# Attention and feed-forward on one core: q and k transposed from the layout in which they were loaded

## The chip, the cores and the metric

The kernel runs on 1 core of one Trainium2 chip. The metric is the device time of one execution in microseconds (us), the median of several runs; lower is better. The time before is 370.84 us, the median of 3 runs (370.76 to 371.65).

## What is computed

Squared-ReLU attention over 8 batches of 12 heads, 448 positions of 64 numbers each, and behind it a feed-forward layer with an exact GELU on the 3,584 tokens. Inputs and output are float32.

```python
# q, k, v: (8, 12, 448, 64); w_in: (768, 2048); w_out: (2048, 768)
scores = (1 / np.sqrt(64)) * np.matmul(q, k.transpose(0, 1, 3, 2))
attn = np.maximum(scores, 0.0) ** 2 / 448
a = np.matmul(attn, v)
x = np.ascontiguousarray(a.transpose(0, 2, 1, 3)).reshape(8 * 448, 12 * 64)
h = x @ w_in
g = 0.5 * h * (1.0 + erf(h / np.sqrt(2)))
out = g @ w_out
```

## The kernel before

Five engines work side by side: TensorE (PE) multiplies, VectorE (DVE) and ScalarE (ACT) empty PSUM, GpSimd (POOL) issues the loads that turn float32 into bfloat16, SyncE (SP) issues stores and DMA transposes. A small scheduler inside the kernel decides, while the program is built, in which order each engine gets its instructions. It keeps estimates of durations and of free buffers, and takes at each step the operation that can start first. The beginning of the program is fixed by a long list, `ORDER`.

Names: `b` is the batch (0 to 7), `g` one of three groups of four heads, `i` one of seven blocks of positions of k, `c` one of four blocks of 112 positions of q.

The scores need q and k with the 64 numbers of a head along the partitions, so both are transposed. For batches 0 and 1, TensorE transposes them by way of PSUM. For batches 2 to 7 a DMA transpose does it, on SyncE's queue, from the tiles `pq` and `pk`, in which the columns of two heads already lie side by side, so that one head lands on partitions 0 to 63 and the other on 64 to 127. Batch 2 is loaded plainly and brought into that layout by VectorE; batches 3 to 7 are loaded into it directly, in pieces of 64 numbers.

```python
# ... batch 2: VectorE permutes what was loaded
def permute_k(copy, g, src):
    copy(get_p()[1][:, g].rearrange("p (i e d) -> p e i d", e=2, d=D),
         src.rearrange("p e (i d) -> p e i d", d=D))
# ... batches 3 to 7: loads straight into the permuted layout (issued from GpSimd)
def add_wide(b):
    def k_fn(e):
        def fn():
            to = get_p()[1].rearrange("p g (i e d) -> e p g i d", e=2, d=D)
            src = kv_view(k, b, 0, G).rearrange("p (g e) (i d) -> e p g i d", e=2, d=D)
            for g in range(G):
                nc.gpsimd.dma_start(to[e][:, g], src[e][:, g])
        return fn
    # ... q the same way, in four parts of three loads; v in one load
# ... DMA transposes of one batch: three for k, four for q
def add_T_dma(b, after):
    for g in range(G):
        # ... nc.sync.dma_start_transpose(kT[:, g], pk[:, g])
    for c in range(NC):
        # ... nc.sync.dma_start_transpose(qT[:, :, bass.ts(c, KC)], pq[:, c, :])
# ... a tiny copy on GpSimd that reads qT: it holds the next batch's loads back
def add_gate(b):
    def fn(e):
        nc.gpsimd.tensor_copy(gate, get_T(b)[0][:, 0, ::KC])
```

A block of scores is four matmuls, one in each quadrant of the array, into one two-bank PSUM tile of a pool of three (`w_pp`). ReLU empties it (ScalarE or VectorE), VectorE squares, and after seven blocks 28 matmuls multiply by v.

```python
ps = box["ps"] = w_pp.tile([128, 2, NB], F32, tag="w", name="ps")
for e in range(2):
    r = slice(64 * e, 64 * e + 64)
    for j in range(2):
        nc.tensor.matmul(
            ps[64 * j : 64 * j + 64, e, x * w : x * w + w],
            kT[r, g, i * 128 + 64 * j : i * 128 + 64 * j + 64],
            qT[r, 2 * g + j, cols(half)], start=True, stop=True)
```

Matmuls of the feed-forward (`psh`, then `pso`, and in the last part `pb`) stand between the attention's in TensorE's order. The second weights come in three loads by rows, `WOUTS = (4, 6, 6)` of sixteen row blocks, the first of them ahead of the transposes of batch 2. VectorE forms sums of their quarters (`t_sb`), with which seven products do the work of eight. `LEADS = {3: 4}` puts four feed-forward runs ahead of batch 3's attention.

Of the kernel before, what the change touches and what calls it, by code (L numbers as in the profile page):

```python
# [8 lines left out]
F32 = mybir.dt.float32  # L9
# [4 lines left out]
KC = 112  # L14
# [9 lines left out]
FF = 2048  # L24
KD = DM // 128
KF = FF // 128
ND = DM // 2
NG = B * S // 256
# [3 lines left out]
WOUTS = (4, 6, 6)  # L32
# [3 lines left out]
T_TWO = 0.72  # L36
# [8 lines left out]
DMA_FREE = 4.54  # L45
# [7 lines left out]
LEADS = {3: 4}  # L53
# [3 lines left out]
NEAR = 0.5  # L57
# [4 lines left out]
WIDE = 2.0  # L62
# [13 lines left out]
G0 G1 G2 G3 G4 G5 A10 D13 G6 A16 P11 P14 G7 D12 A15 P17 G8 D18 P21 P39 D22 P33 P36 A34 D40  # L76
P19 D20 A37 P23 G9 P42 P48 D24 P54 A43 D35 A49 P51 D44 P25 D38 A52 D41 G117 A55 D53 P45 D50
A26 D47 A46 P57 D56 P69 P66 A58 D70 P27 G118 A67 P29 D59 P63 G119 A28 D71 P60 A64 G120 D68
P78 D61 A62 P75 A79 D65 P81 P31 D30 A76 D80 P96 G121 D32 A97 P72 D77 G122 A82 D98 P129 G123
D74 A73 P90 D130 P84 P108 A91 G124 D83 P131 A85 D109 P93 P141 D132 A94 D92 P102 D95 P105  # L80
P111 A103 D86 P143 D110 G125 A106 D104 P99 A112 D107 G126 A144 P87 D100 A101 D113 A142 P157
P114 D88 G127 A158 D89 P133 D115 A116 G128 P135 D159 A134 P160 P163 D136 P166 A164 P145 D167
A161 D165 P253 A146 D168 D162 P169 P172 G147 A254 P175 A173 D170 P245 G148 A176 D171 P255
A246 D177 G149 D174 P184 P187 A256 P196 A185 G150 D188 P137 P139 A138 P178 D197 G151 A140
D186 P193 P211 G152 D180 P247 A212 G153 D213 P249 A248 D179 A194 D198 G154 P263 A250 D195
D229 G155 P223 P220 A264 D189 P190 S235 A224 D221 P265 G156 A191 D225 P267 A266 D192 D222
P199 P217 A268 P214 D231 A218 P257 S236 D215 A200 D219 P259 A258 D216 D201 P181 P208 A260
P205 D230 A209 P261 D182 P251 D183 A262 D210 A206 D233 P202 A252 S237 D207 D232 P226 D234
A203 D204 S238 S239 P269
# [17 lines left out]
class Scheduler:  # L107
# [70 lines left out]
    def commit(self, est, op, eng, dur, lat):  # L178
# [5 lines left out]
        if isinstance(lat, tuple):  # L184
            t = max(self.dma, est + dur + 1.0)
            self.dma = t + lat[0] / 390e3
            op.done = self.dma + DMA_LAT
            self.landed += [op.done] * lat[1]
        else:
            op.done = est + lat  # L190
# [68 lines left out]

    def place(self, fixed):  # L260
# [14 lines left out]
        while rest or any(fixed.values()):  # L275
# [7 lines left out]
            for e, v in fixed.items():  # L283
                if v and not (e == "PE" and by.get("PE")):
                    tops.append(self.pick(v[:1]))
# [11 lines left out]
def kernel(  # L297
# [34 lines left out]
    q32 = natpool.tile([KC, 4, HC * D], F32, tag="pq", name="q32")  # L332
    k32 = natpool.tile([128, 2, NK * D], F32, tag="pk", name="k32")

    def get_nat(b):
        if b not in nq:

            tq, tk = ("pq", "pk") if b == 1 else ("nq", "nk")
            nq[b] = natpool.tile([KC, H, NC * D], BF16, tag=tq, name="nq")
            nk[b] = natpool.tile([128, HP, NK * D], BF16, tag=tk, name="nk")  # L340
            vt[b] = vpool.tile([128, HP, NK * D], BF16, tag="v", name="v_sb")

# [4 lines left out]
    def load_q(b, g0, g1, c0=0, c1=NC):  # L347
        get_nat(b)
        nc.gpsimd.dma_start(  # L349
            nq[b][:, 4 * g0 : 4 * g1, c0 * D : c1 * D], q_view(b, g0, g1, c0, c1)  # L350
        )
# [18 lines left out]
    def load_wout(kf):  # L370
        w = moe_w_out.rearrange("(kf p) d -> p kf d", p=128)
        nc.gpsimd.dma_start(wout_sb[:, kf, :], w[:, kf, :])

    pqk = []

    def get_p():
        if not pqk:  # L380
            pqk.append(natpool.tile([KC, NC, DM], BF16, tag="pq", name="pq"))
            pqk.append(natpool.tile([128, G, NK * 128], BF16, tag="pk", name="pk"))
        return pqk
# [4 lines left out]
    def get_T(b):  # L388
        if b not in qkT:
            qkT[b] = (  # L390
                tpool.tile([128, HP, S], BF16, tag="qT", name="qT"),
                tpool.tile([128, G, NK * 128], BF16, tag="kT", name="kT"),
            )
        return qkT[b]

# [24 lines left out]
    Pq, Pk, Tq, Tk = {}, {}, {}, {}  # L420
# [3 lines left out]
    def war(b):  # L424

        old = [o for (bb, *_), o in list(Pq.items()) + list(Pk.items()) if bb == b - 1]
        c = {1: -1, 2: 0}.get(b, b - 1)
        old += [o[0] for (bb, *_), o in list(Tq.items()) + list(Tk.items()) if bb == c]
        return old

    def add_k(b, g0, g1):
# [4 lines left out]
        o = dma(fn, (g1 - g0) * 4 * S * 256, war(b))  # L436
# [3 lines left out]
    def add_q(b, g0, g1, c0=0, c1=NC):  # L440
# [3 lines left out]
        o = dma(lambda: load_q(b, g0, g1, c0, c1), n, war(b))  # L444
# [4 lines left out]
    def add_v(b, g0, g1):  # L449
        def fn():  # L450
            get_nat(b)
            nc.gpsimd.dma_start(vt[b][:, 2 * g0 : 2 * g1], kv_view(v, b, g0, g1))  # L452

        old = [o for (bb, *_), o in AV.items() if bb == b - 3]
# [4 lines left out]
    def add_wide(b):  # L459


        def k_fn(e):
            def fn():
                to = get_p()[1].rearrange("p g (i e d) -> e p g i d", e=2, d=D)
                src = kv_view(k, b, 0, G).rearrange("p (g e) (i d) -> e p g i d", e=2, d=D)
                for g in range(G):
                    nc.gpsimd.dma_start(to[e][:, g], src[e][:, g])  # L467

            return fn

        def q_fn(e, j):
            def fn():
                to = get_p()[0].rearrange("p c (g j e d) -> j e g p c d", j=2, e=2, d=D)
                src = q[b].rearrange("(g e j) (p c) d -> j e g p c d", e=2, j=2, c=NC)
                for g in range(G):
                    nc.gpsimd.dma_start(to[j][e][g], src[j][e][g])  # L476

            return fn

        def v_fn():  # L480
            vt[b] = vpool.tile([128, HP, NK * D], BF16, tag="v", name="v_sb")
            nc.gpsimd.dma_start(vt[b], kv_view(v, b, 0, G))

        n = G * 4 * S * 256
        ks = [dma(k_fn(e), WIDE * n / 2, war(b), G) for e in range(2)]
        qs = [dma(q_fn(e, j), WIDE * n / 4, war(b), G) for e in range(2) for j in range(2)]
        old = [o for (bb, *_), o in AV.items() if bb == b - 3]
        o = dma(v_fn, n, old)
        ops = Both(ks), Both(qs)
        for g in range(G):  # L490
            ld_v[b, g] = [o]
            Pk[b, g] = ops[0]
            for c in range(NC):
                Pq[b, g, c] = ops[1]

    class Both:


        def __init__(self, ops):
            self.ops = ops  # L500

        @property
        def done(self):
            ends = [o.done for o in self.ops]
            return None if None in ends else max(ends)

    def add_load(b, g0=0, g1=G):
        if b > 2:
            return add_wide(b)
        add_k(b, g0, g1)  # L510
        add_q(b, g0, g1)
        add_v(b, g0, g1)
# [8 lines left out]
    def add_wout(i):  # L521
        m = sum(WOUTS[:i])
        kf = slice(m, m + WOUTS[i])
        ld_wout[i] = dma(lambda: load_wout(kf), DM * 128 * WOUTS[i] * 4)


    def permute_k(copy, g, src):

        copy(
            get_p()[1][:, g].rearrange("p (i e d) -> p e i d", e=2, d=D),  # L530
            src.rearrange("p e (i d) -> p e i d", d=D),
        )

    def permute_q(copy, g, c0, c1, src):

        dst = get_p()[0][:, c0:c1, 256 * g : 256 * g + 256].rearrange(
            "p c (j e d) -> e p j c d", j=2, d=D
        )
        for e in range(2):
            copy(dst[e], src[:, 2 * e : 2 * e + 2].rearrange("p j (c d) -> p j c d", d=D))  # L540

    def add_pk(b, g0, g1, after=(), bias=0.0):
        for g in range(g0, g1):
            deps = ld_k[b, g] + list(after)
            deps += [Tk[max(b - 1, 1), x, i][0] for x in range(G) for i in range(NK)]
            Pk[b, g] = sch.add(
                (("DVE", 0.31, 0.43),),
                lambda e, g=g: permute_k(V.tensor_copy, g, nk[b][:, 2 * g : 2 * g + 2]), deps,
                bias=bias,
            )  # L550

    def add_pq(b, g0, g1, c0=0, c1=NC, after=(), bias=0.0):
        for g in range(g0, g1):
            deps = [ld_q[b, g, c] for c in range(c0, c1)] + list(after)
            deps += [Tq[max(b - 1, 1), g, c][0] for c in range(c0, c1)]
            if b == 2:
                deps += [Tq[1, x, c][0] for x in range(G) for c in range(NC)]
            d = 2 * (0.07 + (c1 - c0) * 128 / 3840)

            def fn(e, g=g):  # L560
                permute_q(
                    V.tensor_copy, g, c0, c1, nq[b][:, 4 * g : 4 * g + 4, c0 * D : c1 * D]
                )

            op = sch.add((("DVE", d, d + 0.12),), fn, deps, bias=bias)
            for c in range(c0, c1):
                Pq[b, g, c] = op
# [89 lines left out]

    xT, hT = {}, {}
# [790 lines left out]
```

## Time and profile before

| | |
|---|---|
| time, median of 3 | 370.84 us (370.76 to 371.65) |
| span of the profiled run | 368.9 us |
| granted TensorE clock | 0.999 |
| PE / DVE / ACT / POOL busy | 358.9 / 288.3 / 200.8 / 108.0 us |
| packets of the loads' queue, share of 16 DMA engines | 58.6% |
| packets of the queue of stores and transposes | 26.8% |

How to read it: busy time is the time in which an engine worked on an instruction. The records of matmuls overlap and their ends are modelled, so a busy TensorE can still lose time; the distance from one start to the next shows that better. PEld is the load of stationary operands, beside the matmuls. In a list of waits, the engine and line that waited stand left of the arrow and what released them right of it, with total us, number of times and the longest. `psh L800` is the tile that is written and the line of the kernel. Idle time of an engine that is not the bottleneck costs nothing.

### The profile page before, as it was taken

The numbers are of one execution on the slowest core, as the hardware profiler recorded it, in microseconds if no ns is written. First come the engines' busy times: TensorE is split into PE (matmuls) and PEld (weight loads), VectorE is DVE, ScalarE is ACT, GpSimd is POOL, SyncE is SP. The second block draws the span as 40 slices with busy tenths as digits, with TensorE's granted clock in tenths as the row PEclk, the third lists the DMA queues.
The fourth block names the chain that finished last, engine by engine and source line by source line (L and its number), as shares of the span: only waits on it lengthen the run. The fifth ranks groups of instructions, "written<-read, shape, count | busy, mean of one in ns | idle before, by whom it ended". The sixth has DMA issues, their size and how long they took to land.

```text
span 368.9 us, 8544 instructions
## 1 busy us (share of the span) xinstructions
PE 358.9 (97%) x3557; PEld 222.1 (60%) x3557; DVE 288.3 (78%) x493; ACT 200.8 (54%) x308; POOL 108.0 (29%) x149
## 2 busy tenths in 40 slices
PE   8799999999999999999999999999999999999994
PEld 7566645455544455544455545457886897688663
DVE  2998991789868978987699888888998658665862
ACT  4988865664447845677755588853440353044200
POOL 8666401726087096097095000000000000000000
PEclk9999999999999999999999999999999999999999
DMA  9999999999999999999999960003002301310233
GB/s 174 196 200 204 202 189 134 173 171 131 244 135 167 160 85 172 209 163 154 146 93 133 205 117 2 3 0 87 2 0 88 85 2 29 109 36 2 85 85 88
DMA packets 114166, 42.98 MB, mean 116 GB/s; under 512 B 92816, under 2 KB 110672, under 8 KB 114128
## 3 DMA queue, kind: packets, MB, share of 16 engines
q0 software_dynamic: 74992, 22.47, 58.6%
q1 hardware_dynamic: 38768, 19.46, 26.8%
q8 instruction: 28, 0.46, 0.5%
q10 hardware_dynamic: 368, 0.51, 0.4%
q14 instruction: 10, 0.08, 0.1%
HBM read 45.61 MB, written 11.01 MB: 153 GB/s over the span
## 4 chain that ended last, share of the span: by engine, by line
PE 87%; DMA 4%; DVE 4%; ACT 2%; POOL 1%; issue 1%; DVEq 0%; POOLq 0%; ACTq 0%
PE pso L1108 32%; PE psh L800 24%; PE pb L942 13%; PE ps L686 8%; PE pav L746 6%; PE pso L1203 3%; DMA v_sb<-in_v_dram 2%; DVE a_sq L707 2%; DMA nk<-in_k_dram 2%; ACT a_sq L698 2%; POOL nk L434 0%; POOL v_sb L452 0%; POOL nq L349 0%; PE tp L580 0%; DVE a_sq L700 0%
## 5 line engine op out<-in xcount | busy, mean ns | idle before, releaser
L698 ACT ACTIVATE a_sq<-ps 128x896 bf16<-128x896 f32 (+1 forms) x136 | 117.4, 914 | 44.6 <-PE ps L686 44.5
L707 DVE TENSOR_TENSOR a_sq<-a_sq 128x896 bf16<-128x896 bf16 (+1 forms) x169 | 97.5, 617 | 7.5 <-ACT a_sq L698 7.2
L800 PE MATMUL psh<-xT,win_sb 128*128 128x448 bf16 (+1 forms) x516 | 96.6, 340 | 0.1
L800 PEld LDWEIGHTS <-win_sb 128*128 128x128 bf16 x516 | 47.8, 98 | 45.5 <-issue 10.2
L810 ACT ACTIVATE h_sb<-psh 128x448 bf16<-128x448 f32 x80 | 43.9, 549 | 24.1 <-PE psh L800 23.9
L1108 PEld LDWEIGHTS <-s_sb 128*128 128x128 bf16 x424 | 40.6, 98 | 27.0 <-issue 2.2
L700 DVE TENSOR_SCALAR a_sq<-ps 128x896 bf16<-128x896 f32 x33 | 35.9, 1090 | 18.3 <-PE ps L686 17.8
L686 PE MATMUL ps<-qT,kT 64*64 64x448 bf16 (+1 forms) x756 | 47.3, 336 | 2.2 <-ACT qT L402 0.6
L976 DVE TENSOR_TENSOR part<-pb,part 128x448 f32<-128x448 f32 x60 | 34.6, 619 | 18.4 <-PE pb L942 18.4
L476 POOL DMA_DIRECT2D pq<-in_q_dram x60 | 41.8, 704 | 10.1 <-DVE a_sq L707 6.4
L1108 PEld LDWEIGHTS <-h_sb 128*128 128x128 bf16 x312 | 29.9, 98 | 21.1 <-issue 2.5
L1108 PE MATMUL pso<-wout_sb,s_sb 128*128 128x384 bf16 (+2 forms) x216 | 38.1, 320 | 0.3 <-DVE osb L1142 0.3
L1108 PE MATMUL pso<-wout_sb,h_sb 128*128 128x384 bf16 x208 | 38.1, 326 | 0.0
L1108 PE MATMUL pso<-t_sb,s_sb 128*128 128x384 bf16 x208 | 38.1, 326 | 0.0
L746 PE MATMUL pav<-a_sq,v_sb 64*64 64x448 bf16 (+1 forms) x756 | 36.8, 330 | 0.7 <-ACT a_sq L698 0.4
L686 PEld LDWEIGHTS <-kT 64*64 64x64 bf16 x756 | 18.3, 105 | 24.2 <-issue 17.4
L985 ACT ACTIVATE h_sb<-part 128x448 bf16<-128x448 f32 x36 | 19.8, 578 | 19.9 <-DVE part L976 19.8
L467 POOL DMA_DIRECT2D pk<-in_k_dram x30 | 28.9, 966 | 1.5 <-issue 0.9
L746 PEld LDWEIGHTS <-v_sb 64*64 64x64 bf16 x756 | 21.1, 107 | 13.0 <-issue 2.3
L942 PEld LDWEIGHTS <-win_sb 128*128 128x128 bf16 x288 | 27.6, 98 | 2.2 <-issue 0.4
L1142 DVE TENSOR_TENSOR osb<-pso,p_sb 128x384 f32<-128x384 f32 x39 | 21.7, 556 | 8.2 <-PE pso L1108 5.7
L400 DVE CAST xT<-pav 128x448 bf16<-128x448 f32 (+1 forms) x43 | 23.7, 583 | 4.6 <-PE pav L746 3.9
(62 smaller groups left out, 292.0 us busy)
## 6 DMA issues: line engine op xcount, KB each, us to landing
pk<-in_k_dram POOLq DMA_DIRECT2D x30, 112.0 KB, 4.4
pq<-in_q_dram POOLq DMA_DIRECT2D x60, 56.0 KB, 5.0
v_sb<-in_v_dram POOLq DMA_DIRECT2D x5, 672.0 KB, 9.1
out_dram<-osb SPq DMA_DIRECT2D x8, 336.0 KB, 3.0
wout_sb<-in_moe_w_out_dram POOLq DMA_DIRECT2D x2, 1152.0 KB, 12.1
v_sb<-in_v_dram POOLq DMA_DIRECT2D x9, 224.0 KB, 8.8
out_dram<-osb SPq DMA_DIRECT2D x7, 288.0 KB, 3.4
out_dram<-osb SPq DMA_DIRECT2D x8, 240.0 KB, 3.1
```

Source lines behind the costliest of these rows:

```text
L467: nc.gpsimd.dma_start(to[e][:, g], src[e][:, g])
L476: nc.gpsimd.dma_start(to[j][e][g], src[j][e][g])
L686: nc.tensor.matmul(ps[64 * j : 64 * j + 64, e, x * w : x * w + w], kT[r, g, i * 128 + 64 * j : i * 128 + 64 * j + 64], qT[r, 2 * g + j, co ...
L698: A.activation(ar, ps, AF.Relu, scale=c_att)
L700: V.tensor_scalar(ar, ps, c_att, 0.0, op0=mybir.AluOpType.mult, op1=mybir.AluOpType.max,)
L707: V.tensor_mul(box["a2"][:, :, :used], ar, ar)
L746: nc.tensor.matmul(pav[0][o2 : o2 + 64, e, :w], vt[b][r, 2 * g + e, bass.ts(i, D)], box["a2"][r, e, o : o + w], start=(i == 0), stop=(i == ...
L800: nc.tensor.matmul(ph[:, x * n : x * n + n], win_sb[:, kd, bass.ts(m + x, 128)], xT[b][:, kd, c], start=(kd == 0), stop=(kd == KD - 1),)
L810: A.activation(h_ring()[:, m : m + nm, o + c.start : o + c.stop], box[0][:, :S].rearrange("p (x n) -> p x n", x=nm), AF.Gelu,)
L942: nc.tensor.matmul(bank[name][:, y, z * HS : z * HS + HS], w[:, k, bass.ts(mm, 128)], right()[:, k], start=first and k == 0 and z == 0, st ...
L976: V.tensor_add(get(to), ps(name), get(other))
L1108: nc.tensor.matmul(box[bank][:, n0:n1], left()[:, kf], right[:, kf, n0:n1], start=bool(need) and kf == 0, stop=kf == K2 - 1, skip_group_ch ...
```

## The change

For batches 2 to 7 the permuted tiles disappear. q and k are loaded plainly, and the DMA transpose reads them as they lie. A block of 128 columns then holds two neighbouring 64-number pieces of the same head, not one piece each of two heads. For k that decides only which piece of which head lands on which half of the partitions. For q, each piece has to be there on both halves, since a piece of k on the upper half needs a q on the upper half. So q is transposed twice, the second time from an offset of 64 columns, with zeros at the ends, into slots that alternate.

Loads and transposes go in turn by groups of four heads: group `g` of the next batch is loaded once group `g` of this one has been transposed. The second weights come in column pieces: first the right half of all rows, then the left half in two steps, all after batch 2's transposes. Tiles move: the two float32 tiles of the start and the inputs of batch 1 use buffers that are free early, and the sums of weights take the space of transposed tiles. The scheduler gets a rule by which a feed-forward run may go ahead of an attention step that would wait, and `LEADS` becomes empty.

```diff
-WOUTS = (4, 6, 6)
+WOUTS = (
+    (slice(ND, DM), [slice(0, KF)]),
+    (slice(0, ND), [slice(0, 4), slice(8, 12)]),
+    (slice(0, ND), [slice(4, 8), slice(12, 16)]),
+)
-LEADS = {3: 4}
+LEADS = {}
 # ... in the scheduler
+    def pick_pe(self, v):
+        top = self.pick(v[:1])
+        wait = math.inf if top is None else top[1] - self.free["PE"]
+        if v[0].mode == "F" or wait <= (PULL if self.mode == "F" else PULL_IN):
+            return top
+        nxt = next((o for o in v if o.mode == "F"), None)
+        other = nxt and self.pick([nxt])
+        if other and other[1] - self.free["PE"] <= PULL and other[1] < self.free["PE"] + wait:
+            return other
+        return top
 # ... permute_k, permute_q, add_pk, add_pq, add_wide are deleted
 # ... in add_T_dma
+        def slots_of(n, o, k):
+            return lambda: get_T(b)[0].rearrange("p (s t) -> p s t", t=KC)[
+                :, 2 * n + o : 2 * (n + k) + o - 1 : 2]
+        def q_src(n, o, k):
+            return lambda: nq[b][:, 128 * n + D * o : 128 * (n + k) + D * o]
+        n0, odd = 0, None
         for g in range(G):
+            op = turn(k_dst(g), k_src(g), list(ld_k[b, g]))
             # ...
+            n = 8 * g + 9
+            even = turn(slots_of(8 * g, 1, 8), q_src(8 * g, 1, 8), lands)
             # ...
+            odd = turn(slots_of(n0, 0, n - n0), q_src(n0, 0, n - n0), lands + beyond)
+            n0 = n
 # ... in the scores
+                            if b < 2:
+                                moving = q_rows(b)[r, 2 * g + j, cols(half)]
+                            else:
+                                n = 4 * (4 * g + 2 * ((2 * i + e) // NK) + j) + 1 - e
+                                moving = qT[r, n * KC : n * KC + S]
 # ... in the order of the program
-    add_load(3)
+    for g in range(G):
+        add_load(3, g, g + 1)
+    add_v(3, 0, G)
 # ...
             if b + 2 < B:
-                add_gate(b + 1)
-                add_load(b + 2)
+                for g in range(G):
+                    add_gate(b + 1, g)
+                    add_load(b + 2, g, g + 1)
+                add_v(b + 2, 0, G)
```

## The prediction

> **What bounds the kernel now.** I read the page's first two parts first, to see which engine is full and where. The columns of the first part are busy time, its share of the span, and instructions; the digits of the second are tenths of a fortieth of the span.
>
> ```profile
> PE 358.9 (97%) x3557; PEld 222.1 (60%) x3557; DVE 288.3 (78%) x493; ACT 200.8 (54%) x308; POOL 108.0 (29%) x149
> ...
> PE   8799999999999999999999999999999999999994
> ...
> DMA  9999999999999999999999960003002301310233
> ```
>
> Two things look full: TensorE to the end, and DMA up to 0.58 of the span. They have to be told apart, because the change is nearly all DMA. The waits of TensorE, longest first in total, decide it:
>
> ```profile
> PE ps L686 <- ACT qT L402: 0.6, 1, 0.6
> ...
> PE tp L580 <- DMA nk<-in_k_dram: 0.4, 1, 0.4
> PE pso L1108 <- DVE osb L1142: 0.3, 1, 0.3
> ...
> PE tp L608 <- DMA nq<-in_q_dram: 0.3, 1, 0.3
> ```
>
> No matmul of the attention waits for a DMA transpose (kT<-pk or qT<-pq), and the two waits for loads, 0.7 us together, are on the TensorE transposes of the first two batches, which the change leaves alone. So the full DMA engines are hidden. The last transposes of the seventh and eighth batch land at 183.3 and 216.5 us (landing times of the transposes), and their first score matmuls run at 190.8 and 221.4 us (chain of waits): 7.5 and 4.9 us in hand. The tightest is the fifth batch: 128.8 against 131.5.
>
> A busy TensorE is not yet one at its peak, so I looked for what is left in the spacing of matmuls, by the timeline of TensorE (start, length, what):
>
> ```profile
> 65.02 0.57 PE L686 MATMUL ps<-qT,kT 64*64 64x448 bf16 x8
> 65.53 1.31 PE L800 MATMUL psh<-xT,win_sb 128*128 128x448 bf16 x6
> 66.76 0.57 PE L686 MATMUL ps<-qT,kT 64*64 64x448 bf16 x8
> 67.27 3.58 PE L800 MATMUL psh<-xT,win_sb 128*128 128x448 bf16 x18
> 70.78 0.76 PE L686 MATMUL ps<-qT,kT 64*64 64x448 bf16 x12
> 71.47 3.58 PE L800 MATMUL psh<-xT,win_sb 128*128 128x448 bf16 x18
> ```
>
> From start to start, 6 full matmuls take 1.23 us and 18 take 3.51, so one takes 2.28/12 = 0.190 and leaving the run costs 3.51 - 18 x 0.190 = 0.09. Eight quadrant matmuls take 0.51 and twelve 0.69, so four (one block of scores) take 0.18 and a visit to the quadrants costs 0.51 - 2 x 0.18 = 0.15 on top. A switch to attention and back is thus about 0.24 us; that is kept by both kernels. The real holes are few:
>
> ```profile
> 96.63 1.52 PE L746 MATMUL pav<-a_sq,v_sb 64*64 64x448 bf16 x28
> 98.50 1.46 PE L1108 MATMUL pso<-wout_sb,s_sb 128*128 128x384 bf16 x8 [0.34 <-DVE osb L1142]
> ```
>
> ```profile
> 151.10 1.49 PE L746 MATMUL pav<-a_sq,v_sb 64*64 64x448 bf16 x28
> 152.42 0.87 PE L686 MATMUL ps<-qT,kT 64*64 64x448 bf16 x8
> 153.22 0.50 PE L1108 MATMUL pso<-t_sb,s_sb 128*128 128x384 bf16 x2
> ```
>
> In the first the 28 matmuls last from 96.63 to 98.50, 1.87 us, where the other runs of 28 take 1.32 plus about 0.1 of a switch: 0.43 lost. In the second eight score matmuls take 153.22 - 152.42 = 0.80 instead of the 0.48 that they take at 76.71 after the same predecessor: 0.32 lost, while ScalarE empties three score tiles in a row and no PSUM buffer is free. The same shape stands at 203.35, 232.95 and 243.68. Together 0.43 + 4 x 0.32 = 1.7 us. That is all that TensorE loses to waits after 60 us. Before 30 us it has more gaps (25.6 busy of 30), in a part that stays as it is.
>
> **What the Trainium skill says.** "Perfetto Trace Analysis", Identifying the Most-Contended Engine, warns that matmul busy time says little about distance from the peak; hence the spacing above, not the 97%. "TensorE: Matmul & The Clock Gate", Back-to-back issue gap, gives N/2.4 + 2.5 ns for one warm matmul, 189 ns for N = 448; the trace agrees with 190, so nothing is to be had inside a run. "DMA: Bandwidth & Descriptors", Specifications, puts full line rate at 512 B and more per piece. The trace agrees in kind: a 128 B packet takes 32 ns and an 896 B one 88 (medians of the packet records), 4.0 against 10.2 bytes per ns. The same page, DMA Transpose (X-bar), has such transposes issued from Sync or Scalar only; here all are on SyncE's queue, in order with the stores, so more of them also means more issue time there.
>
> **The change part by part.**
>
> Matmuls: the changed kernel as built has the same 3,557 matmuls in the same shapes. Query slots are 448 contiguous columns as before, so each matmul should cost the same. Work: 0.
>
> DVE: the three permutes pk<-nk and six pq<-nq of the third batch go.
>
> ```profile
> L540 DVE COPY pq<-nq 112x512 bf16<-112x512 bf16 x6 | 1.4, 287 | 0.0
> ...
> L529 DVE COPY pk<-nk 128x896 bf16<-128x896 bf16 x3 | 1.2, 385 | 0.0
> ```
>
> 1.4 + 1.2 = 2.6 us, all between 40 and 60 us, where TensorE is busy 20.0 of 20 us: 0 on the path.
>
> Loads of the last five batches: the 128 B pieces go.
>
> ```profile
> pk<-in_k_dram POOLq DMA_DIRECT2D x30, 112.0 KB, 4.4
> pq<-in_q_dram POOLq DMA_DIRECT2D x60, 56.0 KB, 5.0
> ...
> qT<-pq SPq DMA_TRANSPOSE x24, 3.8
> ...
> kT<-pk SPq DMA_TRANSPOSE x18, 6.8
> ```
>
> The packet records hold 53,760 packets of 128 B, 112.8 us of all 16 engines, 22.6 us a batch. After: k in 768 pieces of 896 B at 88 ns and q in 1,344 of 512 B at 60 ns, over 16 engines 4.2 + 5.0 = 9.2 us. Saved 13.4 us of engine time a batch. GpSimd issues 6 loads of about 0.73 us where it issued 6 of 0.97 and 12 of 0.70: 4.4 for 14.2 us. None of it is on the path.
>
> Transposes: per batch 3 of 7 blocks and 4 of 6, 45 blocks, become 3 of 7, then 8 + 9 + 8 + 8 + 8 + 8 = 49 for q, 70 blocks in 9 instructions. The 32,256 packets of 256 B take 60.0 us, 10.0 a batch; times 70/45 that is 15.6, so +5.6 us; two more issues at 1.3 us on SyncE. Net DMA per batch: -13.4 + 5.6 = -7.8 us. More slack, where slack was already enough.
>
> Second weights: the first third (768 KB) no longer comes before the third batch's transposes; all 3.1 MB come after. The transposes, which land at 52.8 to 63.4 us now, lose that competitor and the permutes, so the gate should open some 2 or 3 us earlier, near 61. From there 2,048 pieces of 768 B (between the 60 ns of 512 B and the 88 of 896 B, taken as 78) are 10 us for the right half, then 5 + 5 for the left: landing near 72, 77 and 82. The first plain product of the right half runs near 77, the first of the left near 83. It fits, the last with about 1 us.
>
> Order: the fourth batch's attention now starts without four feed-forward groups ahead, some 6 us earlier by the work counted before it (18 psh, 8 pso, 28 pav fewer: 3.4 + 1.3 + 1.3). Its inputs follow the weights: 2.2 us per pair of k and q from 82, so transposes landing near 89 to 95, against a start near 101. The new rule that puts a feed-forward group ahead of a waiting attention step shows as two places where eight scores are split 4, 6 psh, 4. Runs of feed-forward to attention rise from 48 to 50: 2 x 0.24 = 0.5 us more switches.
>
> **Sum.** Holes removed at most 1.7, switches added 0.5: at most -1.2 us. Splitting a hole of 0.32 for a switch of 0.24 gains little; the rest depends on whether the new order hits other full PSUM buffers. I take about three quarters: 370.84 - 0.9 = 369.9 us.
>
> **Rivals.** (1) The left half of the second weights lands late: the four t_sb subtractions and the plain products stall near 80 us, by 1 to 2 us. For it: only 1 us in hand, and DVE waits 2.7 us for this load already. Against: TensorE has attention to run meanwhile, and that 2.7 us made no hole. It would give 371 to 372. (2) DMA was the hidden bound, and its relief speeds up everything. For it: DMA is at 9 tenths to 0.58 of the span. Against: no TensorE wait on a transpose. It would give 363 or less. (3) The doubled q transposes or SyncE's in-order queue become the bound: 9 issues at 1.3 us are 11.7 us of a batch of 30, with stores in between that wait for DVE. Against: 4.9 us or more in hand and 7.8 us less DMA work. A late transpose of 3 us in each of five batches would give 385.
>
> **Range and chances.** The runs before spread from 370.8 to 371.7. Full success with the holes is 369.6, none is 371.3, rival 1 adds to 372, and a little unforeseen gain is allowed below: 368.7 to 371.7. Two per cent is 7.4 us, which the holes cannot give, so faster needs rival 2 (0.02) and slower rival 3 (0.02); 0.96 stays within.
>
> **What would show it right or wrong.** Right: TensorE's waits still hold no transpose; permute lines gone; software queue's share down from 58.6% to near 40%, hardware queue's up from 26.8% to near 36%; digits of DMA below 9 from the middle on; eight score matmuls at 0.48 wherever they follow a run of 28. Wrong: a PE wait on kT, qT or wout_sb, a wider gap near 78 to 84 us, a matmul of 448 columns away from 0.190, or a different time up to 60 us, where I assume nothing moves.

## The result, and the profile after

The changed kernel takes 374.60 us (median of 4 runs, 374.35 to 374.99), the kernel before 371.25 beside it (4 runs, 370.76 to 372.14): a ratio of 1.0088, with a 95% interval of 1.0065 to 1.0112. It is slower by 3.35 us, and outside the range.

First the page of the changed kernel: busy times, the granted clock and the DMA share by fortieths, and the two queues (packets, MB, share of the 16 DMA engines).

```profile
PE 359.7 (96%) x3557; PEld 221.2 (59%) x3557; DVE 282.3 (76%) x480; ACT 204.8 (55%) x312; POOL 63.7 (17%) x101
...
PEclk9999999999989999999999999999999999999999
DMA  9999995999999999999998992002002301310223
...
q0 software_dynamic: 32912, 22.47, 43.8%
q1 hardware_dynamic: 55952, 23.76, 36.2%
```

GpSimd and VectorE have less to do and the loads' queue is emptier, as the change means. TensorE has the same 3,557 matmuls. One digit of the clock is an 8: slice 12, from 102.6 to 111.9 us. To find where the 3.3 us lie, I compared the start times of equal amounts of TensorE work in the two traces. After the first 0.4 us (landing of the first loads) both run level to about 99 us, with a distance between -0.2 and 0.4; then the changed kernel falls back twice, by some 2.3 us up to 102.5 and by 1.9 up to 108, and from there to the end the distance stays between 3.9 and 4.5. The whole loss is one place.

The waits (engine and tile that waited, what released it; total us, times, longest) name it. The two lines of TensorE are its longest, the third is VectorE's.

```profile
PE pso L1086 <- DVE osb L1120: 2.6, 1, 2.6
...
PE tp L530 <- DMA nk<-in_k_dram: 1.0, 2, 0.8
```

```profile
DVE osb L1120 <- DMA out_dram<-osb: 4.1, 2, 3.2
```

There is no wait for a DMA transpose or for `wout_sb`: TensorE waited for VectorE, and VectorE for a *store*. The timeline of the same stretch (start, length, what; the idle time before and its releaser in brackets):

```profile
98.24 1.46 PE L1086 MATMUL pso<-t_sb,s_sb 128*128 128x384 bf16 x8
...
101.69 0.56 DVE L1120 TENSOR_TENSOR osb<-pso,p_sb 128x384 f32<-128x384 f32 x1 [3.19 <-DMA out_dram<-osb]
...
102.30 1.87 PE L1086 MATMUL pso<-t_sb,h_sb 128*128 128x384 bf16 x8 [2.60 <-DVE osb L1120]
```

The feed-forward's results are summed into an output buffer, `osb`, of which there are three. All three were taken: two by the "plain" row blocks (blocks of 128 rows that are multiplied by the second weights before the sums of weights are ready), whose stores had not landed, and one by the other row block of the same group. VectorE takes its instructions in order, so it stood at that addition; TensorE's next product needed the PSUM tile that the addition reads. The chain of waits shows when that store went out:

```profile
97.80 0.53 SPq L1047
...
98.39 3.22 DMA out_dram<-osb
...
101.69 0.57 DVE osb L1120
```

ScalarE's last copy of the first plain row block ran from 87.53 to 88.01 us. The store left at 97.80, ten microseconds later. SyncE's own timeline says why; first the changed kernel, then the one before:

```profile
84.76 1.22 SPq L585 DMA_TRANSPOSE kT<-nk  x1
86.14 1.28 SPq L585 DMA_TRANSPOSE qT<-nq  x1
87.52 7.10 SPq L585 DMA_TRANSPOSE kT<-nk  x1
94.72 2.98 SPq L585 DMA_TRANSPOSE qT<-nq  x1
97.80 1.00 SPq L1047 DMA_DIRECT2D out_dram<-osb  x2
```

```profile
83.30 4.49 SPq L632 DMA_TRANSPOSE kT<-pk  x3
87.89 5.44 SPq L1069 DMA_DIRECT2D out_dram<-osb  x4
```

Before, three k transposes were issued in 4.49 us and the stores followed at 87.89. After, four transposes, k and q in turn, stand ahead of the stores; the third held SyncE for 7.10 us and the fourth for 2.98. One transpose more is ahead, but most of the ten microseconds is that the issue of a transpose has become slow. (The scheduler in the kernel sets this order with an estimate of 1.4 us for an issue, `T_STEP`.)

Why slow? By the packet records, counted per microsecond of time, the transposes of batch 3 (256 B packets) run beside the load of v, in 896 B packets. Between 89 and 92 us there are 159 to 195 transpose packets per us and 154 to 187 load packets, 120 to 154 of them of 896 B and the rest of 512 B: nearly one for one. A load packet of 896 B takes 87 ns there and a transpose packet 31 (medians). At 98 us, with the loads done, there are 1,109 per us, at 18 ns each. In the kernel before, whose loads then were pieces of 128 B, the transposes got 371 to 691 per us (85 to 88 us). The Trainium skill, "DMA: Bandwidth & Descriptors", Queues, rings and completion order, says that a DMA engine takes its queues round-robin, a whole packet (some 9 to 17 descriptors) from each in turn. The counts agree with turns; how many of the records here make one turn, they do not show. A queue of large packets then takes most of the time from one of small packets, and the wider loads of the change hold the transposes up. That the issue stands still because only about two transposes fit ahead of it is an inference from the 1.22, 1.28, 7.10.

The second part of the loss stands in the windows (from:to, length; busy us and instructions of PE, PEld, DVE, ACT, POOL; granted clock; DMA share; GB/s):

```profile
99.40:102.30 2.90, 0.30 (x2) 0.07 (x1) 0.61 (x2) 0.00 (x0) 1.64 (x3) 1.00 0.98 178
102.30:106.40 4.10, 4.10 (x36) 1.89 (x39) 3.71 (x6) 0.92 (x1) 0.00 (x0) 0.61 1.16 115
...
103.20:106.60 3.40, 3.40 (x32) 1.44 (x34) 2.81 (x5) 0.92 (x1) 0.00 (x0) 0.50 1.29 139
```

In the 4.1 us after the idle stretch the clock was 0.61 on average, and this average is made of two values: TensorE first went on for 0.9 us at 1.00, then came 3.4 us at 0.50, in which rounds of four quadrant matmuls started every 365 ns; after them it was every 184. "TensorE: Matmul & The Clock Gate", Why this matters for your kernels, asks for no TensorE gaps over about 3 us; here 2.60 us by the releaser, 2.77 lost from start to start, were enough. (The 2.77 is 2.3 more than the kernel before loses there, since its hole of 0.43 at this place is gone. Gaps in the experiments are from start to start as well, unless a wait is named.)

### The profile page after: what moved, and what is told of

It reads as the page before. It is cut to its first block, busy times and chain, and to the rows that moved or that the text cites. A ratio compares the mean times of both kernels' runs of the same rounds, so it can differ in the third digit from the quotient of the medians.

```text
span 373.0 us, 8450 instructions
## 1 busy us (share of the span) xinstructions
PE 359.7 (96%) x3557; PEld 221.2 (59%) x3557; DVE 282.3 (76%) x480; ACT 204.8 (55%) x312; POOL 63.7 (17%) x101
## 3 DMA queue, kind: packets, MB, share of 16 engines
q0 software_dynamic: 32912, 22.47, 43.8%
q1 hardware_dynamic: 55952, 23.76, 36.2%
## 4 chain that ended last, share of the span: by engine, by line
PE 86%; DMA 5%; SPq 3%; ACT 2%; DVE 1%; POOL 1%; issue 0%; DVEq 0%; POOLq 0%
PE pso L1086 30%; PE psh L772 25%; PE pb L916 13%; PE ps L659 9%; PE pav L720 8%; SPq L585 3%; DMA v_sb<-in_v_dram 2%; DMA nk<-in_k_dram 2%; PE pso L1181 1%; ACT a_sq L671 1%; DMA out_dram<-osb 1%; DVE part L950 1%; POOL nk L471 0%; DVE osb L1120 0%; POOL nq L392 0%
## 5 line engine op out<-in xcount | busy, mean ns | idle before, releaser
L671 ACT ACTIVATE a_sq<-ps 128x896 bf16<-128x896 f32 (+1 forms) x138 | 118.9, 914 | 40.7 <-PE ps L659 40.7
L680 DVE TENSOR_TENSOR a_sq<-a_sq 128x896 bf16<-128x896 bf16 (+1 forms) x169 | 98.2, 616 | 5.3 <-ACT a_sq L671 4.3
L673 DVE TENSOR_SCALAR a_sq<-ps 128x896 bf16<-128x896 f32 x31 | 33.7, 1090 | 28.3 <-PE ps L659 28.1
L720 PE MATMUL pav<-a_sq,v_sb 64*64 64x448 bf16 (+1 forms) x756 | 37.8, 335 | 0.7 <-ACT a_sq L671 0.4
L436 DVE CAST xT<-pav 128x448 bf16<-128x448 f32 (+1 forms) x45 | 24.7, 581 | 3.9 <-PE pav L720 2.6
L626 POOL COPY gate<-qT 128x16 bf16<-128x16 bf16 x13 | 4.4, 336 | 112.0 <-DMA qT<-nq 112.0
L1086 PE MATMUL pso<-t_sb,h_sb 128*128 128x384 bf16 x104 | 19.5, 331 | 2.6 <-DVE osb L1120 2.6
```

What stands on the lines that cost most here:

```text
L436: V.tensor_copy(dst, src)
L671: A.activation(ar, ps, AF.Relu, scale=c_att)
L673: V.tensor_scalar(ar, ps, c_att, 0.0, op0=mybir.AluOpType.mult, op1=mybir.AluOpType.max,)
L680: V.tensor_mul(box["a2"][:, :, :used], ar, ar)
L720: nc.tensor.matmul(pav[0][o2 : o2 + 64, e, :w], vt[b][r, 2 * g + e, bass.ts(i, D)], box["a2"][r, y, o : o + w], start=(i == 0), stop=(i == ...
L1086: nc.tensor.matmul(box[bank][:, n0:n1], left()[:, kf], right()[:, kf, n0:n1], start=bool(need) and kf == 0, stop=kf == K2 - 1, skip_group_ ...
```

## The experiments

Each ratio is to the kernel before, run beside the experiment. My theory: load packets slow the transposes, SyncE's issue stands, the plain stores behind it go late, the third `osb` stays taken, VectorE and TensorE stop, and the clock falls. Rivals: the transposes themselves are what is waited for; the new order of the scheduler makes the gap; the second weights come too late and shift everything.

**1. The plain stores from ScalarE's queue.**

```diff
-lambda e: store_rows(t, osbs[t, "plain"])
+lambda e: store_rows(t, osbs[t, "plain"], queues=[nc.scalar] * 2)
```

> The changed kernel, with the four stores of the two plain row blocks issued from ScalarE instead of SyncE; every other engine keeps its order. Theory A (the stores stand in SyncE's queue behind transposes that issue slowly, so an output buffer is not freed, VectorE waits 3.2 us and TensorE 2.8 us): the stores leave near 90 us, the gap at 99.4 us goes and with it the slow clock after it, so about 4.5 us less than the changed kernel, near 370 to 370.5. Rival B (the late weights or the transposes themselves hold TensorE): the gap stays, 374 to 375.

Measured: 383.52 us (382.26 to 384.9), ratio 1.0337 (1.03 to 1.0373). It misfired. From the timeline, ScalarE's next copy after the store:

```profile
99.10 0.48 ACT L438 COPY osb<-pso 128x384 f32<-128x384 f32 x1 [11.27 <-DMA kT<-nk]
```

The DMAs of these two queues take eight completion semaphores in turn. In the new order the first store got the semaphore last used by a q transpose of batch 3 (issued 86.02, landed 97.95; the releaser in the line, `kT<-nk`, is the profile's inference), had to wait for it, and left at 98.02; ScalarE stood 11.3 us behind it and TensorE 8.7. This says nothing for or against a theory, only that a store moved to an engine that has other work can carry an unseen wait along.

**2. Batch 3's v not loaded** (the kernel uses batch 2's v in its place, so one load is missing).

```diff
+            if b == 3:
+                vt[b] = vt[2]
+                return
```

> The changed kernel without the load of v for the fourth batch (it uses the third batch's v, so 672 KB of loading are left out); all else in the same order. Theory A with its second half (the transposes of the fourth batch issue slowly because the big packets of the loads, v above all, take the DMA engines): the issue of the second k transpose takes under 4 us instead of 7.1, the stores behind it leave by 94 us, and the gap at 99.4 us shrinks from 2.8 us to under 1. Rival C (the doubled q transposes fill SyncE's queue by their number alone): the gap stays over 2 us.

Measured: 370.76 us (one run). The third transpose's issue took 3.63 us instead of 7.10, the stores left at 93.53 instead of 97.80, the first five transposes landed between 91.9 and 98.2 instead of 97.3 and 102.4, and there is no gap at 99 us. The load of v beside the transposes is needed for the gap.

**3. Sixteen idle matmuls in the gap.** The results are used nowhere; they only keep TensorE at work before the product that waits.

```diff
+ # ... d is a PSUM tile; once, ahead of the product that waits
+                for _ in range(16):
+                    nc.tensor.matmul(d[:, 0, :ND], h(1, o2)[:, 0], tsum(4)[:, 0], start=True, stop=True)
```

> The changed kernel with 16 extra matmuls of 384 columns (2.6 us of work, their result unused) in the gap ahead of the product that waits. Theory A says the gap is idle time and about 1.9 us more are lost after it, because the granted clock drops to about 0.6 from 102.3 to 106.4 us. Then the wait for VectorE stays (the product starts near 102.3 as before), but the clock stays at 1.0, and the time falls by 1.7 to 2.1 us to about 372.7. If the slow matmuls after the gap have another cause (their operands come late), the time stays at 374.6 or grows.

Measured: 373.25 us (372.8 to 373.74), ratio 1.0059 (1.0044 to 1.0075). The same two windows:

```profile
99.40:102.30 2.90, 2.90 (x20) 1.74 (x19) 1.24 (x3) 0.00 (x0) 1.46 (x3) 1.00 0.85 131
102.30:106.40 4.10, 4.10 (x56) 2.24 (x55) 4.10 (x8) 1.32 (x2) 0.00 (x0) 1.00 1.27 173
```

VectorE still waits 2.76 us for the store, and the waiting product starts at 101.94, but the clock is 1.00 and 56 matmuls fit where 36 did. That is worth 374.60 - 373.25 = 1.35 us, less than the 1.7 to 2.1 expected: the clock's part is real, and about 1.4 us of the loss (1.7 by equal work in the two traces).

**4. The kernel before, with the changed scheduling rule and the changed `LEADS`.** Loads and transposes as before.

```diff
-LEADS = {3: 4}
+LEADS = {}
+    def pick_pe(self, v):
+ # ... as in the changed kernel, with its constants
```

> The kernel before with only the scheduler's part of the change: the rule that lets a feed-forward run go ahead, its three constants, and no feed-forward runs ahead of the fourth batch; loads, permutes, transposes and weights as before. If the new order is what the changed kernel gains by (holes at full PSUM buffers, at most 1.7 us less 0.5 for switches): 369.6 to 370.6. If the order itself is what makes the output buffers run out near 100 us: a gap there and 372 or more.

Measured: 372.42 us (15 runs, 371.32 to 374.89), ratio 1.0044 (1.0029 to 1.0059). The new order gains 0.65 us up to 100 us, then TensorE waits 1.34 us at 101.94 for `qT`: without the four leading runs batch 3's attention starts before the old transposes have landed (101.81). Another 0.5 us goes at 222 us. So the order has a cost of its own beside the old loads, but it is another wait, and the clock stays at 1.00. It does not make the gap of the changed kernel; the part of the expectation that had the output buffers in it was wrong.

**5. The stores ahead of the transposes, by one dependency.** Only SyncE's order changes: from the third transpose of batch 3 on, each follows the first plain store.

```diff
 # ... stores: the list of the plain stores, in order
-add_T_dma(b + 1, [at(b, n + y // 3) for y in range(9)])
+add_T_dma(b + 1, [at(b, n + y // 3) + (stores[:1] if b == 2 and y > 1 else []) for y in range(9)])
```

> The changed kernel with one edit on SyncE's queue alone: the third and later transposes of the fourth batch stand behind the two stores of the plain row blocks instead of ahead of them; every other engine keeps its order. Theory A (the stores stuck behind a transpose whose issue takes 7.1 us keep the output buffer): the first store leaves at 88 us, VectorE no longer waits for it at 98 us, the gap at 99.4 us and the slow clock after it go: about 4 us less than 374.6, so 370 to 371, if the transposes that are now behind do not land later than the fourth batch's scores need them (about 100 us). Rival B (transposes late for their own sake): the gap only moves, to a wait for qT or kT near 100 us, and the time stays over 372.

Measured: median 371.57 us of 22 runs, ratio 1.0034 (1.0012 to 1.0057). The gap at 99 us is down to 0.31. But the runs lie in two groups, 12 from 370.98 to 371.61 and 10 from 372.6 to 376.6, and the profiled one (375.34) belongs to the second. In it the same thing happens a batch and a half later:

```profile
155.29 0.56 DVE L1120 TENSOR_TENSOR osb<-pso,p_sb 128x384 f32<-128x384 f32 x1 [3.47 <-DMA out_dram<-osb]
```

A store issued at 147.38 among transposes and beside the next v landed at 155.17; TensorE waited 2.11 us, and the clock was 0.58 in the 4.1 us after (0.50 from 156.7 to 160.1). Putting the stores ahead cures the first place; in this run a second one takes over.

**6. Batch 3's v loaded later**, behind the gate of batch 3's first transposes.

```diff
-    add_v(3, 0, G)
+                    if b == 2 and g == 0:
+                        add_v(3, 0, G)
```

> The changed kernel with the fourth batch's v loaded behind the gate that follows its first transposes, instead of ahead of it; every other engine keeps its order. Theory A, second half (the load of v takes the DMA engines from the transposes): as without that load, the second k transpose is issued in under 4 us, the stores leave by 94 us and the gap at 99.4 us goes: 370.5 to 371.5; v lands near 102 us, and may cost up to 1 us of wait there. Rival C (the number of transposes alone fills the queue): issue time stays near 7 us and the gap stays.

Measured: 372.03, 372.11, 376.15 and 376.96 us, ratio 1.0105 (1.0055 to 1.0155). In the profiled run (372.11) the issue took 3.70 us, the stores left at 93.8 and there is no gap at 99. v now lands at 108.4, everything behind it shifts, and at 153 us a store takes 9.15 us to land and TensorE waits 1.3 us. The traffic was moved, not removed.

**7. Batch 3's v in seven loads of 128 B pieces.** The same bytes in packets a seventh as long.

```diff
+ # ... for b == 3
+                for i in range(NK):
+                    nc.gpsimd.dma_start(to[:, :, i], src[:, :, i])
```

> The changed kernel with the fourth batch's v loaded in seven loads of 128-byte pieces instead of one of 896-byte pieces: the same bytes, more engine time in all (about 10.7 us of all 16 engines for 4.2). If the DMA engines take packets of the two queues in turn, so that a 256-byte packet of a transpose waits for one packet of the load whatever its size, the transposes move two to three times as fast beside the small pieces, the second k transpose is issued in under 5 us, and the gap shrinks below 1.5 us although the load itself lasts longer: 371 to 373. If it is the amount of engine time that the loads take, the gap grows: 375 or more.

Measured: 376.34 us (376.09 to 376.74), ratio 1.0141 (1.012 to 1.0162). The theory's first half came out: the transpose's issue fell from 7.10 to 4.16 us, and the packet records between 89 and 92 us hold 333 to 493 load packets and 311 to 378 transpose packets per us, again one for one, twice the transposes of the changed kernel. The second half did not: small packets make the load itself longer, to 103.3 us instead of 97.4, so the transposes further back and the stores behind them are later still (landing 102.0 to 102.7) and the gap is 4.0 us. In these two runs the size of the load's packets sets how fast the transposes move beside it; how long the load lasts still sets when all is done.

**8. The first piece of the second weights ahead of the gate**, as it was before the change.

```diff
+    pool_q[-2:] = pool_q[:-3:-1]
```

> The changed kernel with the first piece of the second weights (right half, 1.5 MB) issued ahead of the gate behind the third batch's transposes, as the kernel before did with its first piece. If the lateness of all that follows the weights is the cause, the fourth batch's loads land some 7 us earlier, its transposes are through before the stores are ready, and the gap at 99.4 us goes: 370 to 371.5. It may cost a new wait at 65 us instead, if the third batch's transposes land later than they do (53.8 us for the first q, 63.1 for the last): then over 372.

Measured: 376.53 us (375.15 to 378.1), ratio 1.0146 (1.0116 to 1.0177). I had expected everything 7 us earlier. The piece competes with batch 2's transposes, which landed up to 71.1 us instead of 63.1; the gate opened later, and the first k transpose went out at 87.92 instead of 84.76. The issue took 6.01 us and the gap was 4.5. This order of the weights is the worse one; but as nothing came earlier, the run does not test whether earlier loads would help. Experiments 10 and 12 bear on that: with loads as late as in the changed kernel the loss is gone.

**9. Transposes allowed one slot later** in the attention of the batch before. Only SyncE's order changes.

```diff
-            n = {2: 2}.get(b, 1)
+            n = {2: 3}.get(b, 2)
```

> The changed kernel with the transposes of each next batch placed one slot (about 5 us) later on SyncE's queue; on every other engine the order is unchanged. Theory A in general (stores that stand behind transposes in SyncE's queue keep the three output buffers, at 99 us in the changed kernel and at 153 us once that gap is gone): stores now mostly come first, both gaps go or shrink below 0.5 us, and the time is 370.5 to 371.5, equal to the kernel before. If transposes then land after their scores need them: a TensorE wait for kT or qT, and over 373.

Measured: median 371.83 us of 22 runs, ratio 1.0022 (1.0006 to 1.0038). The first stores leave at 95.56, still behind a q transpose of 7.0 us, and VectorE waits 1.5 us instead of 3.2. TensorE's gap is 1.1 us, not below 0.5 as expected, and two of the 22 runs are at 376.40 and 378.19. The order helps, by less than the theory said.

**10. Both: stores ahead for batch 3, and the later batches' transposes one slot later.**

```diff
 # ... stores: the list of the plain stores, in order
-            n = {2: 2}.get(b, 1)
-            add_T_dma(b + 1, [at(b, n + y // 3) for y in range(9)])
+            n = 2
+            add_T_dma(b + 1, [at(b, n + y // 3) + (stores[:1] if b == 2 and y > 1 else []) for y in range(9)])
```

> The changed kernel with both edits on SyncE's queue: the stores of the plain row blocks ahead of the fourth batch's later transposes, and the transposes of the later batches one slot later. Theory A: no gap at 99 us and none near 153 us, so the runs near 375 that the first edit alone still had are gone, all between 370.5 and 371.7. Rival: another place in the order takes over, some runs stay at 374 or more.

Measured: 370.65 us (22 runs, 370.13 to 371.80), ratio 0.9989 (0.9978 to 0.9999): 4 us less than the changed kernel, and level with the kernel before (370.98 beside it). SyncE's timeline:

```profile
86.11 1.30 SPq L585 DMA_TRANSPOSE qT<-nq  x1
87.84 5.04 SPq L1047 DMA_DIRECT2D out_dram<-osb  x4
92.97 3.63 SPq L585 DMA_TRANSPOSE qT<-nq  x1
```

The stores leave at 87.84, as in the kernel before, and have landed at 98.6 to 99.7; VectorE waits 0.5 us and TensorE has no gap, neither at 99 us nor at 153. Leaving ten microseconds earlier brings the first row block's landing forward only from 101.6 to 98.7, since two transposes still stand ahead of it in the queue (landed 97.0 and 97.8); 2.9 us are enough. The first six transposes are no earlier for it (97.0 to 107.7 against 97.3 to 107.9). Same matmuls, same loads, same transposes: the order of one queue is worth 4 us.

**11. q transposed once.** The shifted second transposes are left out, and the scores read only half of what they need, in slots that exist.

```diff
-            odd = turn(slots_of(n0, 0, n - n0), q_src(n0, 0, n - n0), lands + beyond)
+            odd = turn(None, None, lands + beyond)
 # ... the scores take the nearest slots that are filled
```

> The changed kernel without the second, shifted transposes of q (3 of 9 per batch; the scores read only slots of the first, so half of q is left out), else in the same order. It prices the doubled q. If the doubling is what makes SyncE's queue too slow: stores leave 3 us earlier or more, the gap at 99.4 us goes, and the time is 370 to 371. If the load traffic beside the transposes alone suffices for the gap: at least 1.5 us of it stay and the time is over 372.

Measured: 370.22 us (20 runs, 370.05 to 371.04), ratio 0.9975 (0.9964 to 0.9985). The stores leave at 89.78 and the gap is gone. With experiment 2 this says that neither the load of v nor the doubled q alone is enough; the gap takes both. (The edit also makes batch 2's transposes fewer, so that batch 3's begin at 80.79 us and not 84.76; the earlier start is part of what it measures.)

**12. The plain row blocks not stored.** Four stores (256 rows of the output) are left out; the transposes stay.

```diff
-lambda e: store_rows(t, osbs[t, "plain"])
+lambda e: None
```

> The changed kernel without the four stores of the two plain row blocks (256 rows of the output are left out). Theory A: nothing holds their two output buffers, the gap at 99.4 us is gone though the transposes land as late as before (97 to 102 us), and TensorE runs on to about 153 us, where the next stores may make a gap of up to 2.5 us. If the transposes' lateness were itself the cause, the gap stays.

Measured: 369.93 us (one run). The third transpose's issue is again 7.10 us, and the transposes land as late as in the changed kernel (the first four at 97.0 to 99.4 against 97.3 to 99.7). Yet:

```profile
98.21 0.56 DVE L1120 TENSOR_TENSOR osb<-pso,p_sb 128x384 f32<-128x384 f32 x1
...
99.31 1.46 PE L1086 MATMUL pso<-t_sb,h_sb 128*128 128x384 bf16 x8
```

The addition that started at 101.69 starts at 98.21 with no wait in front of it. This separates the theories: the late transposes by themselves cost TensorE nothing here; the store that is late behind them makes the gap.

A fourth output buffer, which would be the direct remedy, wasn't tried: four take 12 KB of each partition, and 9.6 are left for them. How much of the loss is the fourth transpose ahead of the stores, and how much the slow third, no run separates.

## Why the prediction was wrong

**Right.** TensorE's bound and the matmuls' cost: 448 columns stay at 0.19 us, and the two traces run level up to 99 us. The permutes and the 128 B pieces gone, worth nothing on the path: the loads' queue at 43.8% and the other at 36.2%, against near 40 and near 36. (The digits of DMA did not fall as foreseen: but for the seventh, a 5, they are 8 or 9 up to 0.6 of the span.) The weights: landed at 75.5 and 77.4 to 83.4, against 72, 77 and 82, with no wait for them, so rival 1 fell. Rival 2 fell as well. The hole at 98.5 us is gone, and of the four holes of 0.32 one is left, at 207.4. The gain of 0.9 us that these holes were to bring is only in part there: with the late stores out of the way experiment 10 takes 370.65, 0.33 less than the kernel before beside it. (Experiment 12, at 369.93, is one run with four stores' work left out.)

**The step that failed** is "two more issues at 1.3 us on SyncE", and with it "More slack, where slack was already enough". An issue took 1.3 us where little stood ahead of it: in the kernel before, batch 3's seven took 1.21 to 1.71. In the changed kernel batch 3's first two took 1.22 and 1.28 too; the next two, behind these and beside loads in packets of 512 and 896 B, took 7.10 and 2.98. Over the whole kernel the 42 issues before add up to 61 us and the 54 after to 123, where twelve more at 1.3 would give 77. The prediction counted the engine time that wider loads save and not whom a long packet holds up, so the change that took load off the DMA engines made the transposes slower where the two meet. Batch 3's landed at 97.3 to 102.4 for the first five and at 107.9 to 115.3 for the other four, against 89 to 95. The kernel before held a sign of it: batch 2's three k transposes, beside loads in pieces of 512 to 1,536 B, took 9.8, 12.0 and 8.6 us from issue to landing.

**The second error** was in what the landing was compared with. Rival 3 named SyncE's in-order queue with "stores in between", and I dismissed it with the slack of the transposes against the *scores* ("4.9 us or more", though the tightest batch in my own working had 2.7). No score matmul waited for a transpose in the end. The slack that counted was the stores' against the output buffers, and I never looked for it. No wait of the kernel before is for a store's landing, so the list of waits is silent; the timelines show it. Before, the same addition was

```profile
99.99 0.56 DVE L1142 TENSOR_TENSOR osb<-pso,p_sb 128x384 f32<-128x384 f32 x1 [0.49 <-PE pso L1108]
```

and the store that frees its buffer had landed at 94.4: 5.6 us in hand. In the changed kernel that store landed 7.2 us later, at 101.6, and VectorE was ready for the addition at 98.5. Rival 3's own figure, 3 us in each of five batches, was wrong as well: it struck once.

**The missing term** is the clock: a gap costs more than itself, because 3.4 of the next 4.3 us ran at half the clock. The experiments split the 3.95 us between the changed kernel and experiment 10: filling the gap gives 374.60 - 373.25 = 1.35, so that is the clock's part, and 373.25 - 370.65 = 2.60 is the gap's. By the comparison of equal work in the traces the clock's part is larger, 1.7 to 1.9.

**What stays open.** Why experiment 5 and, by its spread, 6 fall into two groups of runs, and two runs of experiment 9 stand apart, was not settled; the place at 153 us was seen in the profiles, but not what tips it. That the issue of a transpose blocks at about two in flight is inferred.

## What to carry to other kernels

When a transfer gets longer or slower, check not only who reads it but what stands behind it in the same queue; a store behind a transpose holds an output buffer, and with three buffers and an in-order engine that reaches TensorE. Time saved as a share of the DMA engines is no slack for a queue of small packets: ask which packets run beside it, and take an issue's duration from a stretch with the same neighbours and as much ahead of it in the queue. Order what frees buffers ahead of what only has to be there later; here (experiment 10) that gave 4 us. And ask of each output buffer how long before its next use its store lands.

## What the runs showed of the hardware

TensorE's clock fell to half for 3.4 us after short pauses: after a wait of 2.60 us (changed kernel) and one of 2.11 (experiment 5), each time some 0.3 to 0.9 us after work had begun again; waits of 1.3 us (experiments 4 and 6) left it at 1.00. The issue of one and the same kind of transpose took between 1.2 and 7.1 us, with the traffic beside it and the transposes ahead of it. And DMAs of two issuing engines can wait for each other through the semaphores that they take in turn: 11 us in experiment 1.
